# Folding the features of a 2-D Fourier mixing a second time, with GpSimd row copies and permuted transposes

## The chip, the cores and the metric

The kernel runs on one core of a Trainium2 chip. The core has a matrix engine (TensorE, PE in the profile, with its weight loads listed as PEld), a vector engine (VectorE, DVE), a scalar engine (ScalarE, ACT), GpSimd (POOL) and a queue that issues DMAs (SyncE, SP). Each engine takes its instructions in order and waits on semaphores of the others. The metric is the device time of one execution in microseconds. The kernel before takes 1586.29 us (median of 3 runs, 1585.91 to 1588.53).

## The reference

Attention with a sigmoid instead of a softmax, a Fourier mixing, and a feed-forward block. The shapes are 8 batches, 12 heads, 448 tokens and 64 features per head, so 768 features per token and 3072 in the hidden layer, all in float32:

```python
scores = scale * q @ k.T - log(S)          # per batch and head
x = (1 / (1 + exp(-scores))) @ v           # heads side by side: 448 x 768 per batch
u = x + real(fft(fft(x, axis=tokens), axis=features))
un = (u - mean(u)) / sqrt(var(u) + 1e-6)   # per token
out = u + relu(un @ w_ch1) @ w_ch2
```

The real part of the two-dimensional transform is cos·cos − sin·sin over tokens and features. Both the cosine and the sine have symmetries, so that sums and differences of mirrored rows ("folds") halve a dimension before the tables are multiplied on.

## The kernel before

There are three stages. **Attention and mixing** runs from 0 to about 400 us. Twenty-four groups `gg` (8 batches of 3) hold 4 heads each. A group is 8 time steps `t` of a loop that goes in twos: at part 0 the half-size scores of this group and the last products with v of the group before, at parts 1 to 3 the scores (`scores`, three matmuls of a float32 split in a high part `hi`, made by ScalarE, and a low part `lo`, made by VectorE in `rest`), each followed by a sigmoid on ScalarE. A table `extra` (filled by `at(t, fn)`) says which other work is written into which step: the loads, the casts, the scanning and repacking of the feed-forward weights (`weight`, four VectorE instructions per tile, lines 310 to 319), the folds, and the layer norm of the first 512 tokens (`norm`, with the steps of `norm_plan`). After each step `pin()` fixes the order on every engine, so an engine's order is that of the program text.

**The mixing of a batch** starts when its three groups are done. `values` leaves the attention output transposed in `xT`: six tiles `p` of 128 features (two heads each), each with 2 x 225 tokens, which already are the two mirrored token halves. `fold` works on GpSimd: level 0 adds and subtracts tile `p` and tile `p + 3` (features 384 apart), level 1 the two token halves, and the last level the mirrored tokens; the result goes to `xp`. These are 6 instructions for each of 3 pairs of tiles, 18 for a batch. Then `mix_units(b)` gives a list of TensorE pieces: `stage_d` multiplies with the feature table `cd_sb` (K = 384 features, hence 3 matmuls in a row, for two parities of 193 columns, times 2 x 2 combinations: 24 matmuls `psd` for a batch); ScalarE copies the result to `A`, interleaving the parities; `stage_s` multiplies with the token table (4 matmuls `pss` of 385 columns); VectorE makes the sum `sm` and the difference `df`; `add_x` transposes `xT` back (`psx`, 8 times 3 transposes) and VectorE adds, for the second half of the features with a reversed read of `sm` or `df`, into `u`, which a DMA writes to `u_dram`.

The list holds end marks, and `mix_some()` runs the pieces up to the next mark once per group, at part 2. So three groups in a row carry the **first, second and third section** of a batch's mixing: 13 `psd` and 2 `pss`; 11 `psd` and 9 transposes; 2 `pss` and 15 transposes. The last batch has no groups left to hide in: its pieces alternate with the first up-projections (`psh`) of the next stage, in `mix_rest` and `fill`. The units of a batch are put on the list at step 24 b + 34.

**The plain stage** (to about 590 us) does the feed-forward block of the first 512 tokens while it prepares the weights (`pair`: ScalarE and VectorE split them in two halves, lines 456 and 458, GpSimd makes differences, line 466). **The fast stage** does the other six chunks with seven products instead of eight for each 2 x 2 block. Its matmuls are `psf` and `pso`.

`norm_plan` has ten steps. Step 7 scales the rows (VectorE, line 399), step 8 makes the high half `hl` (ScalarE, line 422), step 9 the low half (VectorE, line 426) and issues two transposing DMAs. `hl` has one buffer. `fx` and `xp` are pools of buffers; `w5` is a one-buffer tag there.

## Time and profile before

| what | value |
|---|---|
| runs | 1586.29 us (1585.91 to 1588.53) |
| the profiled execution | 1584.93 us, its span 1583.2 us |
| mean granted TensorE clock | 0.999 |
| PE busy | 1557.6 us, 98% of the span |
| DVE busy | 1278.7 us, 81% |
| ACT busy | 655.6 us, 41% |
| POOL busy | 319.0 us, 20%, none of it after 570 us |
| DMA | 402.43 MB, 254 GB/s |

A float32 matmul appears as two records in the profile, so the 192 `psd` of the program are 384 records. The records of matmuls are pipelined: the pitch from one start to the next is the time that the engine needs, not the mean duration of one record. Some records are missing. In a timeline a row merges neighbouring equal instructions, "x24" gives their number, and the bracket says how long the engine idled before the row and who ended it. In a view of one source line three numbers with slashes are the shortest, the median and the longest instance in nanoseconds.

### The profile page before, as it was taken

How to read it: one execution, taken by the hardware profiler on the slowest of the kernel's cores; microseconds unless marked ns; L12 is line 12 of the kernel's file. 1: busy time of each engine (PE TensorE's matmuls, PEld its weight loads, DVE VectorE, ACT ScalarE, POOL GpSimd, SP SyncE). 2: the span in 40 equal slices, each digit the busy share in tenths (PEclk: the TensorE clock that was granted, in tenths of full speed). 3: DMA queues.
4: the chain of work that ended last, by engine and by line, in shares of the span. 5: the costliest groups of instructions: out<-in, count | busy, mean ns of one | idle time of the engine just before them, and what ended most of it. 6: DMA issues, size and time to landing. Idle time of an engine off the chain costs nothing.

```text
span 1583.2 us, 27410 instructions
## 1 busy us (share of the span) xinstructions
PE 1557.6 (98%) x11059; PEld 1063.7 (67%) x11059; DVE 1278.7 (81%) x2354; ACT 655.6 (41%) x780; POOL 319.0 (20%) x244
## 2 busy tenths in 40 slices
PE   8999999899999999999999999999999999999998
PEld 3556565465555557777777777777777777777775
DVE  4997788793799956887888888888788878877778
ACT  8777777674555424222232233232423232223221
POOL 3644343255788920000000000000000000000000
PEclk9999999999999999999999999999999999999999
DMA  7888878792788977668657766866676777576571
GB/s 296 305 315 275 311 263 296 268 302 88 278 281 295 317 306 291 201 238 303 234 190 291 252 232 229 306 205 253 255 257 196 280 285 241 165 293 255 198 272 50
DMA packets 130399, 402.43 MB, mean 254 GB/s; under 512 B 68832, under 2 KB 70112, under 8 KB 111712
## 3 DMA queue, kind: packets, MB, share of 16 engines
q1 hardware_dynamic: 130272, 400.68, 71.0%
q8 instruction: 86, 1.41, 0.3%
q14 instruction: 41, 0.34, 0.1%
HBM read 311.39 MB, written 73.92 MB: 243 GB/s over the span
## 4 chain that ended last, share of the span: by engine, by line
PE 67%; DVE 4%; DMA 1%; issue 1%; ACT 1%; POOL 1%; SPq 0%; DVEq 0%; ACTq 0%; POOLq 0%
PE pso L897 29%; PE psf L841 29%; PE po L625 4%; PE psh L605 3%; DVE wp L458 1%; DMA ws<-w_dram 1%; DVE F L847 1%; POOL wq L466 1%; DMA U<-u_dram 0%; DVE H L847 0%; ACT H L876 0%; DVE ur L646 0%; DVE ur L925 0%; DVE acc L974 0%; DVE acc L912 0%
## 5 line engine op out<-in xcount | busy, mean ns | idle before, releaser
L841 PE MATMUL psf<-ut,ws 128*128 128x256 f16 x4536 | 506.6, 273 | 2.3 <-DVE ur L646 1.2
L897 PE MATMUL pso<-ws,H 128*128 128x384 f16 x3024 | 503.4, 326 | 1.0 <-DVE H L847 0.9
L841 PEld LDWEIGHTS <-ws 128*128 128x128 f16 x4536 | 443.2, 98 | 62.2 <-issue 1.7
L897 PEld LDWEIGHTS <-H 128*128 128x128 f16 x3024 | 295.3, 98 | 190.2 <-DVE H L847 1.7
L866 ACT ACTIVATE F<-F 128x1024 f32<-128x1024 f32 x72 | 76.1, 1057 | 406.6 <-DVE F L847 406.6
L912 DVE TENSOR_TENSOR acc<-pso,acc 128x384 f32<-128x384 f32 x399 | 207.9, 551 | 19.6 <-PE pso L897 19.6
L847 DVE TENSOR_TENSOR H<-F,H 128x1024 f16<-128x1024 f32 (+1 forms) x144 | 155.4, 1088 | 48.8 <-ACT H L876 48.5
L876 ACT ACTIVATE H<-F 128x1792 f16<-128x1792 f32 x72 | 122.2, 1697 | 110.7 <-DVE F L847 110.7
L127 ACT ACTIVATE a<-sc 128x900 f32<-128x900 f32 x168 | 147.1, 920 | 47.9 <-PE sc L139 47.0
L847 DVE TENSOR_TENSOR F<-X,psf 128x256 f32<-128x256 f32 x288 | 117.2, 419 | 59.3 <-PE psf L841 54.7
L466 POOL TENSOR_TENSOR wq<-wq 128x384 f32<-128x384 f32 x96 | 148.7, 1555 | 37.6 <-DVE wp L458 31.9
L847 DVE TENSOR_TENSOR F<-F 128x256 f32<-128x256 f32 x288 | 109.5, 422 | 24.8 <-ACT F L866 20.1
L177 PE MATMUL av<-a,vr 128*64 128x450 f32 x576 | 119.1, 550 | 0.0
L458 DVE SCALAR_TENSOR_TENSOR wp<-wq,wsc,wp 128x1536 f16<-128x1536 f32 x48 | 98.5, 2085 | 20.7 <-ACT wp L456 20.7
L847 DVE TENSOR_TENSOR X<-X,psf 128x256 f32<-128x256 f32 x216 | 89.9, 416 | 19.0 <-PE psf L841 17.5
L605 PE MATMUL psh<-ut,wp 128*128 128x512 f16 x432 | 98.5, 379 | 0.0
L197 POOL TENSOR_TENSOR eo<-xT 128x450 f32<-128x450 f32 x48 | 53.3, 1132 | 209.3 <-ACT xT L185 209.3
L855 ACT ACTIVATE X<-psf 128x256 f32<-128x256 f32 x72 | 27.8, 386 | 156.4 <-PE psf L841 156.4
L625 PE MATMUL po<-wp,hh 128*128 128x256 f16 (+1 forms) x384 | 88.6, 326 | 0.0
L456 ACT ACTIVATE wp<-wq,wsc 128x1536 f16<-128x1536 f32 x48 | 73.4, 1569 | 27.7 <-DMA wq<-t_dram 25.9
L177 PEld LDWEIGHTS av<-a,vr 128*64 128x64 f32 x576 | 37.2, 136 | 69.1 <-issue 69.1
L605 PEld LDWEIGHTS <-wp 128*128 128x128 f16 x432 | 42.2, 98 | 49.4 <-issue 0.7
(91 smaller groups left out, 1604.6 us busy)
## 6 DMA issues: line engine op xcount, KB each, us to landing
ws<-w_dram SPq DMA_DIRECT2D x144, 1344.0 KB, 7.6
wr<-w_in SPq DMA_DIRECT2D x48, 768.0 KB, 7.8
w_dram<-wp SPq DMA_DIRECT2D x24, 1344.0 KB, 9.9
qk<-qk_in SPq DMA_DIRECT2D x23, 898.0 KB, 6.0
t_dram<-wt SPq DMA_DIRECT2D x48, 384.0 KB, 7.1
wq<-t_dram SPq DMA_DIRECT2D x24, 768.0 KB, 6.5
vr<-v_in SPq DMA_DIRECT2D x24, 448.0 KB, 4.6
U<-u_dram SPq DMA_DIRECT2D x24, 384.0 KB, 9.2
```

Source lines behind the costliest of these rows:

```text
L127: nc.scalar.activation(a, ps[:, :, :SQ], AF.Sigmoid, bias=-math.log(S), scale=1.0 / math.sqrt(D))
L177: nc.tensor.matmul(ps[j * D:(j + 1) * D, :SQ], vr[:, h:h + D], a[:, j], start=False, stop=(c == 2))
L458: nc.vector.scalar_tensor_tensor(out=w[:, 1, part], in0=t, scalar=sc, in1=w[:, 0, part], op0=ALU.mult, op1=ALU.subtract)
L466: nc.gpsimd.tensor_tensor(out=t[:, o], in0=t[:, x], in1=t[:, y], op=op)
L605: nc.tensor.matmul(hs[c, f], l[:, m], r[:, m], start=(m == n == 0), stop=(m == NCC - 1 and n == 2))
L625: nc.tensor.matmul(po[n][:, at:at + hi - lo], l[:, cols], r[:, lo:hi], start=(f == 0 and m == 0 and at == 0), stop=(f == NFC - 1 and m == ...
L841: nc.tensor.matmul(ps[:, :TH], w[:, x, a, m * 128:(m + 1) * 128], ut[y][:, b, m], start=(m == n == 0), stop=(m == n == 2))
L847: nc.vector.tensor_tensor(out=o, in0=x, in1=y, op=op)
L866: nc.scalar.activation(F[:, 0:4], F[:, 0:4], AF.Relu)
L876: nc.scalar.activation(hts[P][:, 0], F[:, 1:8], AF.Copy)
L897: nc.tensor.matmul(ps[:, :384], H[:, x, a, tp * 128:(tp + 1) * 128], w[:, y, b], start=(j == n == 0 and half != 1), stop=(j == 1 and n == ...
L912: later(0, lambda: nc.vector.tensor_tensor(out=to, in0=ps[:, :384], in1=to, op=ALU.add))
```

## The change

It has four parts.

1. **The features are folded once more.** The host permutes the heads (`HEADS`), the features of four heads of v, and the rows and columns of the weights and of the result (`_columns`), so that mirrored features meet in one partition. `fold` gets a level 2 that combines pair 2 with pair 1. K falls from 384 to 256, so `stage_d` has 2 matmuls in a row instead of 3 (16 for a batch), and its table has two parities of 198 columns instead of 193 (`NL` = 396). The `pss`, `A`, `Q`, `sm` and `df` have 396 columns instead of 385.
2. **GpSimd copies rows.** The fold leaves four rows in the wrong partition (0 or 64). `turn_rows` rotates them with four copies of 1 x 900 elements for each batch.
3. **Permuted transposes replace column handling.** The second half's transposes multiply with a permuted identity (`perm`, a new DMA of 128 x 384) and the tables hold the columns in the order wanted. ScalarE's copy to `A` is now contiguous, and the reads of `sm` and `df` are runs of 64 columns and not a reversed row.
4. **The norm's halves come later**: steps 8 and 9 at 23 + 16 j and 25 + 16 j instead of 19 + 8 j and 22 + 8 j. The row of the weight scan takes the `w5` buffer, and `weight_row` moves from step `TP` + 2 to `TP` + 4.

The order of the folds changes with `FOLDS`: the last level of pairs 0 and 1 now stands behind the row copies, and pair 2 has eight instructions. On GpSimd the first batch reads as follows before (`eo` is level 0, `fd` level 1, `xp` the result):

```order
L197 TENSOR_TENSOR eo<-xT 128x450 x2
L200 TENSOR_TENSOR fd<-eo 128x450 x2
L203 TENSOR_TENSOR xp<-fd 128x4x113 x2
L197 TENSOR_TENSOR eo<-xT 128x450 x2
L200 TENSOR_TENSOR fd<-eo 128x450 x2
L203 TENSOR_TENSOR xp<-fd 128x4x113 x2
L197 TENSOR_TENSOR eo<-xT 128x450 x2
L200 TENSOR_TENSOR fd<-eo 128x450 x2
L203 TENSOR_TENSOR xp<-fd 128x4x113 x2
```

and as follows after the change:

```order
L206 TENSOR_TENSOR eo<-xT 128x450 x2
L209 TENSOR_TENSOR fd<-eo 128x450 x2
L206 TENSOR_TENSOR eo<-xT 128x450 x2
L209 TENSOR_TENSOR fd<-eo 128x450 x2
L223 COPY eo<-fd 1x900
L223 COPY fd<-fd 1x900 x2
L223 COPY fd<-eo 1x900
L215 TENSOR_TENSOR xp<-fd 128x4x113 x2
L206 TENSOR_TENSOR eo<-xT 128x450 x2
L209 TENSOR_TENSOR xp<-eo 128x450 x2
L212 TENSOR_TENSOR xp<-xp,fd 128x2x225
L212 TENSOR_TENSOR xp<-xp,fd 128x450
```

followed by the two last-level instructions of pair 2. There are 18 tensor instructions as before and four copies; behind the last `xT` of the batch stand eight instructions and not six.

On TensorE the first section of the first batch, between the scores, reads before:

```order
L139 MATMUL sc<-hi,lo 128x450 x2
L216 MATMUL psd<-cd_sb,xp 113x193 x12
L227 MATMUL pss<-A,cs_sb 113x385
L216 MATMUL psd<-cd_sb,xp 113x193
L227 MATMUL pss<-A,cs_sb 113x385
```

and after:

```order
L144 MATMUL sc<-hi,lo 128x450 x2
L235 MATMUL psd<-cd_sb,xp 113x198 x8
L245 MATMUL pss<-A,cs_sb 113x396
L235 MATMUL psd<-cd_sb,xp 113x198
L245 MATMUL pss<-A,cs_sb 113x396
```

Four `psd` have left; the second section loses four as well.

On ScalarE the first high half `hl` of the norm stands before between the cast of the weights (`wt`) and the copy of a group's attention output, a few instructions ahead of the mixing's copies `A`:

```order
L127 ACTIVATE a<-sc 128x900
L185 ACTIVATE xT<-av 128x450
L127 ACTIVATE a<-sc 128x900 x2
L305 ACTIVATE wt<-wr 128x768
L422 ACTIVATE hl<-un 128x768
L185 ACTIVATE xT<-av 128x450
```

and after, half a group later, behind them:

```order
L239 ACTIVATE A<-psd 113x396 x2
L132 ACTIVATE a<-sc 128x900 x2
L120 ACTIVATE hi<-qk 128x898
L324 ACTIVATE wt<-wr 128x768
L441 ACTIVATE hl<-un 128x768
L132 ACTIVATE a<-sc 128x900
```

It moved past a section of the mixing, and the second of the two stands 16 steps behind the first instead of 8.

The diff, cut to its core:

```diff
-FOLDS = ((12, 13, 14, 15, 16, 17), (20, 21, 22, 23, 24, 25), (28, 28, 28, 29, 29, 29))
+FOLDS = ((12, 0, 0), (13, 0, 1), (14, 0, 2), (15, 0, 3), (20, 1, 0), (20, 1, 1), (21, 1, 2), (21, 1, 3), (27, 0, 6), (27, 0, 7),
+         (28, 2, 0), (28, 2, 1), (28, 2, 2), (28, 2, 3), (29, 2, 4), (29, 2, 5), (29, 2, 6), (29, 2, 7))
+NB = 66
+NL = 6 * NB
...
-            cd_sb = c1.tile([128, 2, 2, 3, 193], F32, name="cd_sb")
+            cd_sb = c1.tile([128, 2, 2, 2, NL // 2], F32, name="cd_sb")
+            perm = c1.tile([128, 3, 128], F32, name="perm")
...
                 elif lv == 1:
-                    eo, fd = eos[p]
-                    e.tensor_tensor(out=fd[:, n], in0=eo[:, :, 0], in1=eo[:, :, 1], op=op)
+                    eo = eos[p]
+                    e.tensor_tensor(out=fd[:, 2 * n:2 * n + 2], in0=eo[:, :, 0], in1=eo[:, :, 1], op=op)
+                elif lv == 2:
+                    k = slice(1, 3) if n else slice(0, 4, 3)
+                    e.tensor_tensor(out=fd[:, k], in0=fd[:, k], in1=fds[b][:, 1, k], op=op)
                 else:
-                    fd = eos[p][1]
+                    fd = fd.rearrange("p (c r) n -> p c r n", c=2)
                     e.tensor_tensor(
-                        out=xp[:, n, :, :, p], in0=fd[:, :, :, 0:HM], in1=fd[:, :, :, HS - 1:HM - 2:-1], op=op)
+                        out=xp[:, n, :, :, 1 - p // 2], in0=fd[:, :, :, 0:HM], in1=fd[:, :, :, HS - 1:HM - 2:-1], op=op)
+
+            def turn_rows(b, n):
+
+                z, y = fds[b][:, 0], fds[b][:, 1]
+                s = eos[1].rearrange("p k r n -> p (k r) n")
+                o, x = ((s[64:65], y[64:65]), (y[64:65], y[0:1]), (y[0:1], z[64:65]), (z[64:65], s[64:65]))[n]
+                nc.gpsimd.tensor_copy(out=o, in_=x)
...
                     nc.tensor.matmul(
-                        ps[:HM, par * 193:par * 193 + 193], xp[:, kp ^ c, c, par, p],
-                        cd_sb[:, c, par, p], start=(p == 0), stop=(p == 2))
-                    if par == 1 and p == 2:
+                        ps[:HM, par * NL // 2:(par + 1) * NL // 2], xp[:, kp ^ c, c, par, p],
+                        cd_sb[:, c, par, p], start=(p == 0), stop=(p == 1))
+                    if par == 1 and p == 1:
                         act_next.append(lambda: nc.scalar.activation(
-                            A[:, kp, c].rearrange("s (i r) -> s r i", r=2),
-                            ps[:HM, 0:386].rearrange("s (r i) -> s r i", r=2), AF.Copy))
+                            A[:, kp, c], ps[:HM, 0:NL], AF.Copy))
...
-                        ps[:m, :385], cs_sb[:HM, kp, c, :m], A[:, kp, c, :385], start=True, stop=True)
+                        ps[:m, :NL], cs_sb[:HM, kp, c, :m], A[:, kp, c], start=True, stop=True)
...
-                    for i in range(3):
+                    for i, (j, n) in enumerate((((0, 0), (1, 0), (2, 0)), ((3, 1), (5, 2), (4, 2)))[hf]):
                         nc.tensor.transpose(
-                            ps[:HM - kp, i * 128:(i + 1) * 128], xT[:, hf * 3 + i, r, kp:HS:2], ident)
-                    y = d if hf == r else s
+                            ps[:HM - kp, i * 128:(i + 1) * 128], xT[:, j, r, kp:HS:2], perm[:, n])
-                    ysl = y[:m, 384:0:-1] if hf else y[:m, 0:384]
+                    y = (d if hf == r else s)[:m].rearrange("s (r b k) -> s b r k", r=2, k=NB)
+                    y = y[..., 0:64] if hf else y[..., 2:66]
...
-                    return [(0.33, lambda par=par, p=p: stage_d(kp, c, par, p)) for par in range(2) for p in range(3)]
+                    return [(0.33, lambda par=par, p=p: stage_d(kp, c, par, p)) for par in range(2) for p in range(2)]
...
-                    for n, t in ((1, 10), (7, 17), (8, 19 + 8 * j), (9, 22 + 8 * j)):
+                    for n, t in ((1, 10), (7, 17), (8, 23 + 16 * j), (9, 25 + 16 * j)):
...
+                for n in range(4):
+                    at(24 * b + 22, lambda b=b, n=n: turn_rows(b, n))
```

More of the change, by code (lines that the diff above doesn't have):

```diff
@@ L26 @@
 CP = 128
+HEADS = [0, 5, 4, 3, 1, 2, 6, 11, 10, 9, 7, 8]
 CH = 64
@@ L543, in spectral_attention_ffn @@
             at(17, lambda: nc.sync.dma_start(cd_sb, cd))
-            at(22, lambda: (nc.sync.dma_start(cs_sb, cs), nc.sync.dma_start(ident, ident_in)))
+            at(22, lambda: (nc.sync.dma_start(cs_sb, cs), nc.sync.dma_start(ident, ident_in[:, 0]),
+                            nc.sync.dma_start(perm, ident_in[:, 1:])))
             ends = sorted([(t, (-10, -5, -1, 0, 3)) for t in range(15, TP, 8)]
@@ L1027, in _layout @@
     B = q.shape[0]
+    q, k, v = (a[:, HEADS] for a in (q, k, v))
+    v = v.copy()
+    for h in (2, 3, 8, 9):
+        v[:, h] = v[:, h][..., -np.arange(D) % D]
+    w1, w2 = w1[_columns()], w2[:, _columns()]
     qt, kt = (a.reshape(B, 2, NG, 2, S, D).transpose(0, 2, 1, 3, 5, 4).reshape(B, 2 * NG, 2 * D, S) for a in (q, k))
@@ L1060, in _layout, with _heads, _places, _columns @@
     return {"qk_in": qk, "v_in": vt, "w1_in": w1t, "w2_in": w2t, "cd_in": cd, "cs_in": cs,
-            "id_in": np.eye(128, dtype=np.float32)}
+            "id_in": np.stack([np.eye(128, dtype=np.float32)] + [
+                np.eye(128, dtype=np.float32)[:, p.ravel()] for p in _places()], axis=1)}
+def _heads():
+    import numpy as np
+    r = np.arange(64)
+    p = np.arange(128)
+    return np.stack([np.concatenate([r, 320 + r]), np.where(p % 64, 320 - p, 256 - p), 64 + p])
+def _places():
+    import numpy as np
+    res = np.zeros((3, 2, 64), int)
+    for k in range(2):
+        core = np.array([n for n in range(2, 128) if n % 64 > 1 and n % 2 == k])
+        ends = np.array([k, 64 + k])
+        res[0, k] = np.concatenate([core, ends])
+        res[1, k] = np.concatenate([(128 - ends) % 128 if k else ends, 128 - core])
+        res[2, k] = np.concatenate([ends, core])
+    return res
+def _columns():
+    import numpy as np
+    l, p = _heads(), _places()
+    half = [l[b][p[0].ravel()] for b in range(3)]
+    return np.concatenate(half + [384 + l[b][p[n].ravel()] for b, n in ((0, 1), (2, 2), (1, 2))])
 def _tokens():
```

56 lines of the change are left out of this document (32 added, 24 removed).

## The prediction

> **What bounds the kernel now.** I read the busy shares first, then the chain that ended last, then how the stage that the change touches looks in a timeline of TensorE, and the waits of that stage.
>
> ```profile
> PE 1557.6 (98%) x11059; PEld 1063.7 (67%) x11059; DVE 1278.7 (81%) x2354; ACT 655.6 (41%) x780; POOL 319.0 (20%) x244
> PE 67%; DVE 4%; DMA 1%; issue 1%; ACT 1%; POOL 1%; SPq 0%; DVEq 0%; ACTq 0%; POOLq 0%
> ```
>
> TensorE is busy for 98% of the span and carries the chain of waits. Whether the attention stage, the first 400 us, is bound by it too is read from its rhythm. These rows, from the timeline of TensorE, are the half-size scores that open every third group, each at the same place of a batch:
>
> ```profile
> 81.60 0.93 PE L152 MATMUL sc<-qk 64*64 64x450 f32 x8
> 128.71 0.94 PE L152 MATMUL sc<-qk 64*64 64x450 f32 x8
> 175.80 0.94 PE L152 MATMUL sc<-qk 64*64 64x450 f32 x8
> 223.65 0.94 PE L152 MATMUL sc<-qk 64*64 64x450 f32 x8
> 271.56 1.22 PE L152 MATMUL sc<-qk 64*64 64x450 f32 x7
> 324.39 1.00 PE L152 MATMUL sc<-qk 64*64 64x450 f32 x8
> ```
>
> Two batches take 47.11 and 47.09 us, equal to 0.02 us: TensorE sets the pace and nothing interrupts it. The next three take 47.85, 47.91 and 52.83, so something does there. Behind 400 us no edit changes an instruction of the main loop, and I take it as moved, not changed. So the gain is what TensorE gets rid of in the attention stage, plus those interruptions, minus what VectorE and GpSimd do to it.
>
> **The matmuls.** This is the first section of a batch:
>
> ```profile
> 105.14 4.19 PE L216 MATMUL psd<-cd_sb,xp 128*113 128x193 f32 x24
> 109.17 0.81 PE L227 MATMUL pss<-A,cs_sb 113*113 113x385 f32 x2
> 109.82 0.49 PE L216 MATMUL psd<-cd_sb,xp 128*113 128x193 f32 x2
> L216 PE MATMUL psd<-cd_sb,xp x384: 323/327/420, 57.7 to 399.4; 128*113 128x193 f32 x192
> ```
>
> From start to start, 24 records of `psd` take 109.17 − 105.14 = 4.03 us, 0.168 us each, and 2 records of `pss` take 0.65 us, 0.325 each. (The means of single records overlap and aren't used.) The slope is (0.325 − 0.168) / (385 − 193) = 0.00082 us per column. Of 384 records of `psd` 128 go: −21.5 us. The 256 that stay get 5 columns: 256 x 0.0041 = +1.05 us. The 64 records of `pss` get 11 columns: 64 x 0.009 = +0.6 us. Sum: **−19.9 us**, 2.5 us per batch, 1.25 in each of two sections.
>
> Of the **last batch** half is not earned. Its pieces run among the first up-projections, and there TensorE waits for something that the change doesn't touch:
>
> ```profile
> 377.52 1.92 POOL L197 TENSOR_TENSOR eo<-xT 128x450 f32<-128x450 f32 x2 [5.72 <-ACT xT L185]
> 381.52 2.08 POOL L203 TENSOR_TENSOR xp<-fd 128x452 f32<-128x452 f32 x2
> 384.15 2.13 PE L216 MATMUL psd<-cd_sb,xp 128*113 128x193 f32 x12
> 389.76 3.04 ACT L456 ACTIVATE wp<-wq,wsc 128x1536 f16<-128x1536 f32 x2 [2.92 <-DMA wq<-t_dram]
> 393.25 0.90 PE L227 MATMUL pss<-A,cs_sb 113*113 113x385 f32 x2 [2.73 <-ACT A L220]
> ```
>
> GpSimd finishes `xp` at 383.60, half a microsecond ahead of the first `psd`. With two more instructions of 0.98 behind the last `xT` it finishes 2 us later, and `psd` starts some 1.6 us late. Yet four pieces further `pss` stands at 393.25 behind two weight casts of 3.04 us on ScalarE, which wait for a DMA. The lateness and the shorter first section both vanish in that wait of 2.73 us: **+1.3 us** (nothing, if the DMA lands earlier; 2.6, if the row copies below are at their upper price).
>
> **The norm's halves.** These rows, ScalarE and TensorE mixed, lie in the long batches:
>
> ```profile
> 216.71 0.84 ACT L422 ACTIVATE hl<-un 128x768 f16<-128x768 f32 x1 [2.60 <-DVE un L399]
> 220.91 0.59 PE L248 MATMUL psx<-ident,xT 128*113 128x128 f32 x3 [0.55 <-ACT A L220]
> 281.45 0.84 ACT L422 ACTIVATE hl<-un 128x768 f16<-128x768 f32 x1 [2.80 <-DVE un L399]
> 285.62 0.90 PE L248 MATMUL psx<-ident,xT 128*112 128x128 f32 x3 [1.93 <-ACT Q L231]
> 300.58 0.84 ACT L422 ACTIVATE hl<-un 128x768 f16<-128x768 f32 x1 [3.28 <-DMA ut<-hl]
> 304.78 0.90 PE L227 MATMUL pss<-A,cs_sb 113*113 113x385 f32 x2 [1.53 <-ACT A L220]
> 271.00:304.00 33.00, 29.61 (x181) 16.66 (x181) 27.22 (x41) 21.43 (x29) 7.91 (x9) 0.95 0.67 218
> ```
>
> The last is the row of that stretch, with the granted clock at 0.95. Three times ScalarE stands for 2.6 to 3.3 us in front of the high half `hl`, for a scaling that VectorE hasn't done or for the transposing DMAs that still read the one buffer; what is queued behind it (the copies `xT`, `Q` and `A`) comes late, and TensorE waits. The cost is 47.85 − 47.10 = 0.75 and 52.83 − 47.10 = 5.73 us, **−6.5 us** in all. The 0.8 us of the batch from 223.65 is another wait (VectorE's small norm instructions, not moved) and stays. After the change `hl` comes six steps behind the scaling (before: two), and the second 16 steps behind the first (before: eight), two thirds of a batch of 47.1 us, so 31 us. The 0.84 us of work stays on ScalarE, which is busy for 23 of 33 us there (the row from 172 us below): nothing. Bounds: 2 us if one of the waits only moves, 7.3 if the 0.8 goes as well.
>
> **VectorE in the first 90 us.** A gain of TensorE is only kept while the others can follow:
>
> ```profile
> 20.00:57.00 37.00, 35.63 (x244) 16.12 (x240) 31.18 (x32) 32.21 (x42) 25.14 (x18) 1.00 0.86 323
> 57.00:74.00 17.00, 16.96 (x108) 10.09 (x108) 16.69 (x21) 11.31 (x17) 8.68 (x6) 1.00 0.82 283
> 74.00:90.00 16.00, 16.00 (x115) 10.16 (x111) 15.61 (x20) 12.75 (x18) 8.50 (x7) 1.00 0.93 309
> 172.00:205.00 33.00, 32.51 (x214) 19.35 (x212) 28.25 (x46) 23.36 (x31) 14.09 (x14) 1.00 0.86 319
> PEld sc L139 <- DVE lo L123: 0.7, 2, 0.3
> L319 DVE SCALAR_TENSOR_TENSOR wt<-wr,wt x48: 957/958/1728, 29.2 to 351.4; 128x768 int32<-128x768 int32 x48
> L310 DVE TENSOR_SCALAR_CACHE_REDUCE wt<-wt x48: 937/945/949, 25.9 to 347.5; 128x768 f32<-128x768 f32 x48
> L197 POOL TENSOR_TENSOR eo<-xT x48: 976/983/1752, 22.0 to 378.5; 128x450 f32<-128x450 f32 x48
> ```
>
> The columns of the first rows are the stretch, its length and the busy times of PE, PEld, DVE, ACT and POOL. From 57 to 90 us VectorE is busy for 32.3 of 33 us; later for 28 of 33. The scores already wait for its low parts (0.7 us, twice). So what TensorE saves in the first section of the first batch, 1.25 us, is lost: that is the lower bound. The upper bound comes from GpSimd. VectorE's instructions with two inputs from SBUF take 0.96 us alone and up to 1.73 beside GpSimd, whose own go from 0.98 to 1.75; line 310, with one input, never slows down. So the two share something, and each microsecond of GpSimd can cost VectorE 0.77/0.98 = 0.8. Between 36 and 57 us GpSimd gets two level-2 instructions (2.0 us) and four row copies.
>
> A **row copy** of 900 elements in one partition is nowhere in the trace. From below it is the 0.10 us of GpSimd's start-up fills; from above twice the 0.98 of a `tensor_tensor` with 450 results. I take 1.0: a copy of 900 reads as many words as that instruction does. That makes 6.0 us more on GpSimd, 4.8 for VectorE if all of it collides; I take six tenths, since about that share of VectorE's time there is two-input work: 2.7. With the 1.3 it is **+4 us** (1.3 to 6; to 9 with copies of 2 us).
>
> The Trainium skill, page "GPSIMD Engine Reference", section "Specifications", says that GpSimd's way to SBUF is shared with VectorE and that instructions of VectorE with two SBUF inputs contend; the rows above agree, and this speaks against putting copies there. Its section "Elementwise — side-by-side cycle accounting" gives about 1.03 cycles per element for one input against 2.6 for two: an estimate by that page of 0.8 us for a copy, by which this term would be 3.6 us instead of 4; no run here shows it yet.
>
> In later batches the fold has room:
>
> ```profile
> 75.29 2.63 POOL L197 TENSOR_TENSOR eo<-xT 128x450 f32<-128x450 f32 x2 [8.58 <-ACT xT L185]
> 89.48 2.58 POOL L197 TENSOR_TENSOR eo<-xT 128x450 f32<-128x450 f32 x2 [6.06 <-ACT xT L185]
> 94.13 2.09 POOL L203 TENSOR_TENSOR xp<-fd 128x452 f32<-128x452 f32 x2
> ```
>
> The last pair starts at 89.48 and `psd` at 105.14: 15.7 us for eight instructions of 1.0 to 1.3. GpSimd idles 6 to 9 us before each pair, more than four copies of 1 us.
>
> **Hand-offs.** With `psd` shorter, ScalarE's copy `A` has less cover:
>
> ```profile
> 106.31 0.95 ACT L115 ACTIVATE hi<-qk 128x898 fp32r<-128x898 f32 x1
> 107.40 0.53 ACT L220 ACTIVATE A<-psd 113x386 f32<-113x386 f32 x1
> ```
>
> The first four `psd` will end at about 106.7, but `hi` holds ScalarE to 107.26; `A` ends at 107.8, and the `pss` that reads it is due at 105.14 + 8 x 0.344 = 107.9. No wait, or 0.2 us: **+0.7 us** for seven batches (0 to 1.5). The contiguous copy, the eleven columns on VectorE and its runs of 64 lie on engines with slack after 90 us; the table's DMA shrinks by 732 words per row, the permutations add 384. I cost these at nothing; without slack 64 additions of perhaps 0.05 us more would be 3 us.
>
> **The sum**: −19.9 + 1.3 − 6.5 + 4 + 0.7 = −20.4 us. The span goes from 1583.2 to 1562.8 us and the profiled execution from 1584.93 to 1564.5. The median of the runs lies 1.4 us above the profiled one, so 1586.3 − 20.4 = **1566 us**. The bounds all at once give 1560 (−26) and 1577 (−9); the forecast's own range is 1560 to 1573, without the upper price of the copies.
>
> **Rivals.** *GpSimd's collisions decide*: copies of 2 us (its upper bound) make the early term 9 us, and the batches after it lose 1 us each: 20.4 − 5 − 7 = 8.4 us gain, 1578. For it: two engines that visibly slow each other, and VectorE at 86% (28.25 of 33). Against it: that leaves it 4.75 us of slack in 33, and four copies come once in 47. *The norm's wait only moves*: `hl` keeps its one buffer. Gain 13.9, 1572. *VectorE catches up at once*: no early loss but 1.3, no hand-off waits: gain 24, 1562 or a little below. *Slower*: from the `xT` of pair 1 (75.29) to `psd` (105.14) there are 29.9 us, 28.5 with the shorter section, for 14 tensor instructions of about 1.25 and four copies: up to (28.5 − 17.5) / 4 = 2.75 us per copy nothing happens; above it each microsecond costs 4 us per batch, because `psd` waits for GpSimd. The gain of 2.5 per batch and 0.8 from the norm is used up at 3.6 us; at 4 us eight batches lose 40 us, less the gain, and the kernel takes about 1604. For it: no GpSimd copy and no one-partition instruction in the trace. Against it: nothing on GpSimd takes over 2.6 us, collisions included. *The change doesn't do what it says* has nothing for it: the order lists show 16 `psd` per batch.
>
> **Chances.** My forecast (1560 to 1573) 0.67, collisions 0.12, the norm's wait moved 0.09, catching up 0.08, slower 0.04. The range that leaves out two tenths at most is 1560 to 1577. A measurement here tells 0.2%, 3 us, from no change. Faster 0.94, the same 0.02, slower 0.04.
>
> **What would show it.** Right: the opening rows of a batch 44.6 us apart from about 120 us on; no idle time in front of ScalarE's `hl`; copies near 1 us; waits of the scores for `lo` of 2 to 4 us before 75 us. Wrong: `psd` waiting for GpSimd in every batch, a pitch of `psd` that doesn't follow the columns (0.172 us per record is expected), a new idle time in front of `pss`, or a longer main loop behind 400 us.

## The result, and the profile after

The change makes the kernel slower: **1598.55 us** (median of 4 runs, 1596.05 to 1603.23) against 1586.1 us for the kernel before on the same chip, a ratio of 1.0081 (95% interval 1.0066 to 1.0097). The forecast was 1566 us. The profiled execution is the slowest of the four, 1603.23 us with a span of 1601.5 us, 18.3 us more than before, so its stretches show more than the 12.5 us between the medians.

The page of the changed kernel, TensorE's busy time and the granted clock in 40 slices:

```profile
PE 1551.6 (97%) x10931; PEld 1052.8 (66%) x10931; DVE 1304.5 (81%) x2354; ACT 655.0 (41%) x780; POOL 374.3 (23%) x276
PEclk9999998899999999999999999999999999999999
```

TensorE has 128 records less, VectorE is busy 26 us longer with the same 2354 instructions, and GpSimd 55 us longer, with 32 copies more. Before, no slice had a clock below 9 tenths. The opening scores of every third group, from the timeline of TensorE after the change:

```profile
81.95 0.93 PE L157 MATMUL sc<-qk 64*64 64x450 f32 x8
130.86 0.93 PE L157 MATMUL sc<-qk 64*64 64x450 f32 x8
178.66 0.94 PE L157 MATMUL sc<-qk 64*64 64x450 f32 x8
226.44 0.93 PE L157 MATMUL sc<-qk 64*64 64x450 f32 x8
289.74 1.58 PE L157 MATMUL sc<-qk 64*64 64x450 f32 x8
342.29 0.93 PE L157 MATMUL sc<-qk 64*64 64x450 f32 x8
```

Batches of 44.6 us from 120 us on were forecast. They take 47.8, 47.8, 63.3 and 52.6 us; before it was 47.1, 47.9, 47.9 and 52.8. The first `psh` starts 16.6 us later than before (396.86 against 380.26), so the loss lies in the attention stage. What TensorE saves in the first and second section is there: groups of 15.35 and 14.34 us stand where 16.56 and 15.59 stood. The third section gives it back, and two single places add more.

**The third section.** VectorE, GpSimd and TensorE after the change, in the group from 130.86 us (`lo` is the scores' low part, `wt` a weight tile, `u` the mixing's addition; the bracket is idle time and who ended it):

```profile
131.24 0.94 DVE L329 TENSOR_SCALAR_CACHE_REDUCE wt<-wt 128x768 f32<-128x768 f32 x1
132.22 1.30 DVE L333 TENSOR_SCALAR wt<-wt 128x768 int32<-128x768 int32 x1
133.55 1.70 DVE L336 SCALAR_TENSOR_TENSOR wt<-wr,wt 128x768 int32<-128x768 int32 x1
135.28 1.70 DVE L338 SCALAR_TENSOR_TENSOR wt<-wr,wt 128x768 int32<-128x768 int32 x1
141.82 1.62 DVE L338 SCALAR_TENSOR_TENSOR wt<-wr,wt 128x768 int32<-128x768 int32 x1
143.37 0.55 DVE L275 TENSOR_TENSOR u<-psx,df 113x384 f32<-113x384 f32 x1
129.44 2.67 POOL L223 COPY fd<-fd 1x900 f32<-1x900 f32 x2
132.17 0.93 POOL L223 COPY fd<-eo 1x900 f32<-1x900 f32 x1
133.18 2.99 POOL L215 TENSOR_TENSOR xp<-fd 128x452 f32<-128x452 f32 x2
138.73 2.24 POOL L206 TENSOR_TENSOR eo<-xT 128x450 f32<-128x450 f32 x2 [2.56 <-ACT xT L191]
143.97 2.03 PE L266 MATMUL psx<-perm,xT 128*112 128x128 f32 x9 [2.30 <-DVE u L275]
```

The whole group, before (first) and after; the columns are the stretch, its length, the busy time and count of PE, PEld, DVE, ACT and POOL, the granted clock, the DMA share and GB/s:

```profile
128.71:143.65 14.94, 14.44 (x100) 7.78 (x96) 11.67 (x19) 10.78 (x15) 5.92 (x6) 1.00 0.89 300
130.86:148.95 18.09, 15.79 (x99) 8.95 (x95) 17.75 (x23) 10.98 (x15) 15.08 (x12) 0.91 0.80 300
```

GpSimd is busy for 15.1 of 18.1 us where it was 5.9 of 14.9, and VectorE has no room left. VectorE's weight instructions with two inputs take 1.70 us and not 0.96, line 333 takes 1.30 and not 0.56; line 329 keeps its 0.94. So two weight tiles end at 143.4, `u` comes late, and TensorE's transposes, which need the PSUM bank that `u` frees, stand for 2.30 us. Nothing like it stood here before. (Pair 1 has no last level of its own any more, so only pair 0's stands behind the copies.)

The Trainium skill, page "SBUF — State Buffer", section "Who interferes with whom", describes this: VectorE and GpSimd share one pair of ports as an exclusive lock, wanted by VectorE's instructions with two SBUF inputs and by a `tensor_scalar` in its two-port form, but not by the one that writes an accumulator, while ScalarE has ports of its own. The trace agrees in each case (lines 336, 333, 329; ScalarE's is below).

**The clock.** The same place by stretches, with the same columns:

```profile
141.60:143.90 2.30, 0.07 (x1) 0.00 (x0) 2.27 (x4) 0.34 (x1) 2.30 (x2) 1.00 1.05 430
143.90:146.00 2.10, 2.03 (x11) 1.69 (x11) 2.00 (x6) 0.00 (x0) 1.94 (x3) 0.59 1.00 413
146.00:147.20 1.20, 1.20 (x6) 1.09 (x8) 1.20 (x3) 0.00 (x0) 1.12 (x2) 0.50 1.05 435
147.20:148.20 1.00, 1.00 (x12) 0.62 (x9) 1.00 (x2) 0.68 (x1) 1.00 (x1) 0.76 0.93 389
```

After 2.3 us of waiting TensorE runs at 0.5 to 0.76 of its clock for 4.3 us. The third section takes 18.09 us against 14.94 before: 3.15 us, of which the wait is 2.3.

**The norm.** SyncE, VectorE, ScalarE and TensorE after the change, in the batch of 63.3 us:

```profile
255.73 0.41 SPq L341 DMA_DIRECT2D t_dram<-wt  x1
270.20 0.95 DVE L445 TENSOR_TENSOR hl<-un,hl 128x768 f16<-128x768 f32 x1
271.19 0.38 SPq L427 DMA_DIRECT2D un<-u_dram  x1
277.79 0.89 ACT L324 ACTIVATE wt<-wr 128x768 f32<-128x768 f32 x1 [9.42 <-DMA wr<-w_in]
279.17 0.98 PE L266 MATMUL psx<-perm,xT 128*113 128x128 f32 x3 [5.31 <-ACT xT L191]
284.72 0.98 PE L266 MATMUL psx<-perm,xT 128*113 128x128 f32 x3 [4.57 <-DVE u L275]
```

SyncE issues nothing for 15 us. `un` has one buffer. The second pair's load stands at step 96 + 32 + 4 = 132, and the low half that reads the buffer last (line 445) now stands at 96 + 25 + 16 = 137, no longer at 126. The load waits for it, the weights' loads wait behind the load, ScalarE stands for 9.4 us, and this group takes 27.4 us against 16.0. ScalarE's waits in front of `hl` are gone, as forecast.

### The profile page after: what moved, and what is told of

Read it like the earlier page. It is cut to its first block, busy times and chain, and to the rows that moved or that the text cites. A ratio compares the mean times of both kernels' runs of the same rounds, so it can differ in the third digit from the quotient of the medians.

```text
span 1601.5 us, 27187 instructions
## 1 busy us (share of the span) xinstructions
PE 1551.6 (97%) x10931; PEld 1052.8 (66%) x10931; DVE 1304.5 (81%) x2354; ACT 655.0 (41%) x780; POOL 374.3 (23%) x276
## 4 chain that ended last, share of the span: by engine, by line
PE 60%; DVE 9%; DMA 3%; ACT 2%; issue 1%; POOL 1%; SPq 0%; ACTq 0%; DVEq 0%; POOLq 0%
PE psf L862 26%; PE pso L918 25%; PE po L646 4%; PE psh L626 3%; DVE F L868 2%; DMA ws<-w_dram 1%; DVE wp L477 1%; DVE H L868 1%; ACT H L897 1%; DVE acc L933 1%; ACT F L887 1%; DMA U<-u_dram 1%; DVE X L868 1%; POOL wq L485 1%; DMA wq<-t_dram 0%
## 5 line engine op out<-in xcount | busy, mean ns | idle before, releaser
L933 DVE TENSOR_TENSOR acc<-pso,acc 128x384 f32<-128x384 f32 x399 | 207.5, 549 | 19.9 <-PE pso L918 19.9
L477 DVE SCALAR_TENSOR_TENSOR wp<-wq,wsc,wp 128x1536 f16<-128x1536 f32 x48 | 98.9, 2091 | 20.5 <-ACT wp L475 15.2
L868 DVE TENSOR_TENSOR X<-X,psf 128x256 f32<-128x256 f32 x216 | 89.6, 415 | 19.6 <-PE psf L862 17.6
```

Source lines behind the costliest of these rows:

```text
L477: nc.vector.scalar_tensor_tensor(out=w[:, 1, part], in0=t, scalar=sc, in1=w[:, 0, part], op0=ALU.mult, op1=ALU.subtract)
L868: nc.vector.tensor_tensor(out=o, in0=x, in1=y, op=op)
L933: later(0, lambda: nc.vector.tensor_tensor(out=to, in0=ps[:, :384], in1=to, op=ALU.add))
```

## Experiments

The kernel before had medians of 1585.1 to 1587.0 us beside these. The last five columns are starts in the timeline of TensorE: the first scores of four groups, named by where they stand in the kernel before, and the first `psh`. Runs that are not in the table stand in the text. From the first `psh` to the end the profiled executions take 1200.9 to 1205.9 us, though no edit touches the main loop and of the mixing only the last batch lies there, so a difference of a few microseconds between two times needn't lie in the attention stage.

| kernel | us | ratio to before (95%) | 128 us | 175 us | 223 us | 356 us | `psh` |
|---|---|---|---|---|---|---|---|
| before | | | 128.71 | 175.80 | 223.65 | 356.14 | 380.26 |
| after | 1598.55 | 1.0081 (1.0066–1.0097) | 130.86 | 178.66 | 226.44 | 373.20 | 396.86 |
| a_norm_back | 1598.57 | 1.0084 (1.0067–1.0101) | 129.87 | 177.63 | 226.94 | 368.44 | 392.44 |
| b_norm_late | 1589.74 | 1.0028 (1.0016–1.0040) | 128.97 | 176.06 | 223.16 | 362.17 | 386.29 |
| a_no_copies | 1578.83 | 0.9962 (0.9947–0.9976) | 125.21 | 169.84 | 219.15 | 351.14 | 375.12 |
| a_old_order | 1580.30 | 0.9967 (0.9956–0.9979) | 125.32 | 169.95 | 220.99 | 352.39 | 376.31 |
| a_norm_mid | 1594.24 | 1.0051 (1.0036–1.0066) | 130.78 | 178.56 | 226.35 | 364.88 | 388.51 |
| a_mid_no_copies | 1577.08 | 0.9941 (0.9927–0.9956) | 124.28 | 168.93 | 213.60 | 347.94 | 371.56 |
| a_weight_170 | 1572.72 | 0.9912 (0.9897–0.9927) | 124.07 | 168.95 | 213.62 | 346.33 | 369.98 |
| b_copies | 1600.33 | 1.0085 (1.0068–1.0102) | 132.70 | 179.79 | 227.63 | 370.93 | 395.05 |
| a_copies_act | 1598.32 | 1.0076 (1.0060–1.0093) | 132.39 | 180.75 | 229.06 | 367.52 | 391.46 |
| a_behind_q | 1588.36 | 1.0012 (1.0002–1.0021) | 131.02 | 177.24 | 223.81 | 358.69 | 383.14 |
| a_rows_early | 1586.99 | 1.0001 (0.9989–1.0013) | 128.91 | 174.35 | 220.26 | 355.24 | 379.89 |
| a_rows_best | 1587.44 | 1.0000 (0.9992–1.0009) | 126.61 | 171.85 | 217.81 | 354.96 | 379.59 |

### Which part of the change costs

The norm alone, put back in the changed kernel (`a_norm_back`) and put into the kernel before (`b_norm_late`):

```diff
-for n, t in ((1, 10), (7, 17), (8, 23 + 16 * j), (9, 25 + 16 * j)):
+for n, t in ((1, 10), (7, 17), (8, 19 + 8 * j), (9, 22 + 8 * j)):
```

> The changed kernel with the norm's steps 8 and 9 at their old places. Theory 1 (the loss is the norm's: the load of the second pair of rows shares one buffer with the rows whose low half is now later, and SyncE's queue stands behind it for some 15 us): the group that took 27.4 us in the changed kernel falls back to about 16.5, the three waits of ScalarE before the high half (6.5 us) come back, and the stall near 333 us goes if it is a consequence: 1588 us, or 1593 if that stall stays. Rival (the norm's move is a gain of 6.5 us as predicted, and all of the loss lies in the fold): 1605 us.

> The kernel before with only the norm's steps 8 and 9 at their new places. Theory 1: the load of the rows is queued on SyncE behind the late low half here too, 11 us lost at that place and up to 5 behind it against 6.5 gained: 1591 to 1596 us. Rival (the move is the gain that was predicted): 1580 us.

In the kernel before the move costs 4.7 us, where 6.5 us of gain were forecast; the blocked group takes 27.5 us there too. In the changed kernel putting it back gains nothing, neither the 1588 us of theory 1 nor the rival's 1605: the blocked group falls to 17.7 us as theory 1 said, but groups of 21.9 and 19.6 us come up behind it, where ScalarE waits 5.1 us for the transposing DMAs of `hl` and TensorE 3.1 us for a late `u`. So the block is real, and most of the loss lies elsewhere.

The copies, and the order that they bring (both on top of `a_norm_back`; `a_old_order` also puts pair 0's last level at steps 16 and 17):

```diff
-                for n in range(4):
-                    at(24 * b + 22, lambda b=b, n=n: turn_rows(b, n))
```

> The changed kernel with the norm at its old places and without the four GpSimd row copies: four rows of the folded features stay in the wrong partition, so part of the mixing is left out. Theory 2 (GpSimd's copies collide with VectorE in the third section of a batch, VectorE's additions u come 2 to 4 us late, TensorE waits and its clock drops): the waits of the third section's transposes for u are gone, and 3 us for each of seven batches: 20 to 25 us under the kernel with the norm alone put back, 1563 to 1568. Rival (the order: pair 0's last level and pair 2's eight instructions stand in the third section with or without copies): half of the wait stays, 8 to 12 us less, about 1578. Second rival (the permuted transposes or the additions in runs of 64 are slow by themselves): no change, 1588.

> As the kernel without copies, and pair 0's last level stands right behind its first two levels, as in the kernel before. Theory 2 (the copies): the same time as without copies, within 3 us. Rival (the order): another 8 to 12 us less, because GpSimd has 2 to 3 us less to do in the third section.

**The copies cost 19.7 us**, just under the 20 to 25 us that theory 2 expected; the order by itself costs nothing (1580.3 against 1578.8). That 1578.83 us is also the first rival's 1578 is luck: both counted from a kernel of 1588 us, and that took 1598.57. The third section without copies, GpSimd and VectorE:

```profile
124.23 2.96 POOL L215 TENSOR_TENSOR xp<-fd 128x452 f32<-128x452 f32 x2
133.15 2.68 POOL L206 TENSOR_TENSOR eo<-xT 128x450 f32<-128x450 f32 x2 [5.96 <-ACT xT L191]
132.09 0.96 DVE L336 SCALAR_TENSOR_TENSOR wt<-wr,wt 128x768 int32<-128x768 int32 x1
133.08 0.96 DVE L338 SCALAR_TENSOR_TENSOR wt<-wr,wt 128x768 int32<-128x768 int32 x1
135.06 0.56 DVE L275 TENSOR_TENSOR u<-psx,df 113x384 f32<-113x384 f32 x1 [1.03 <-PE psx L266]
```

GpSimd's idle 5.96 us are VectorE's undisturbed ones: the last weight instruction ahead of `u` ends 8.8 us after the group's first scores (134.04 − 125.21), with copies 12.6 us (143.44 − 130.86). VectorE has 1.0 us to spare and loses 3.8. The regular batch takes 44.63 us, the 44.6 of the forecast, so no cost of the permuted transposes or of the additions in runs of 64 is seen.

The same four copies in the kernel before, into a free row:

```diff
+                for n in range(4):
+                    at(24 * b + 26, lambda b=b, n=n: more_copies(b, n))
```

> The kernel before with four GpSimd copies of 1 x 900 elements for each batch, from a row of fd to a free row of eo, in the step behind pair 1's last level, where GpSimd idled for 9 us; the computation is unchanged. Theory 2: VectorE's instructions beside them stretch by 0.8 to 1 us for each copy, 3.2 to 4 us; VectorE had 2.25 us to spare before u, so 1 to 2 us are lost for each of seven batches: 1594 to 1600 us. Rival (copies in GpSimd's idle time are free, as the prediction had it, and the loss belongs to the other edits): 1586 us.

15.2 us. The timeline shows where: in the regular batches nothing is lost (14.93 and 14.94 us for the third sections from 132.7 and 179.8 us). VectorE had more to spare there in the kernel before, as its timeline shows, and GpSimd had the last level of pair 1 behind it:

```profile
138.55 0.56 DVE L255 TENSOR_TENSOR u<-psx,df 113x384 f32<-113x384 f32 x1 [2.25 <-PE psx L248]
```

The 15.2 us are lost in the first batch (3.8 us in its first section) and behind 227 us, where the norm adds to VectorE's work. So the time just above the expected 1594 to 1600 us is luck: the loss of 1 to 2 us in each of seven batches did not come.

### Taking the norm's block away, and what then remains

`a_norm_mid` writes steps 8 and 9 at 23 + 10 j and 25 + 10 j, so that the last low half (step 131) stands ahead of the load (132). `a_mid_no_copies` is that without copies, and `a_weight_170` has in addition

```diff
-          + [(t, (-10, -2, -1, 0, 3)) for t in (34, 58, 82, 154, 162, 178)])
+          + [(t, (-10, -2, -1, 0, 3)) for t in (34, 58, 82, 154, 170, 178)])
```

> The changed kernel with the norm's steps 8 and 9 at 23 + 10 j and 25 + 10 j: as late as in the change for the first half, but the last low half is written one step ahead of the load of the next rows. Theory 1 (the load that stands on SyncE behind the low half is the norm's whole loss, ScalarE's waits are the gain): the 27.4 us group falls to about 16, ScalarE doesn't wait before the high half, 11 us less than the changed kernel and 16 with the stall near 333 us: 1583 to 1588 us. Rival (with VectorE late from the collisions, some wait before the high half comes back as it did with the old places): 1594 to 1598 us.

> The same without GpSimd's four row copies; four rows stay in the wrong partition, so part of the mixing is left out. Theory 2: this is the gain that was predicted, matmuls 19.9 and norm 6.5 us less 1.3, 0.7 and what is left of VectorE's early lateness: 1562 to 1568 us. Rival (the norm's waits move elsewhere also without collisions): 1574 to 1579 us.

> The kernel with the norm at 23 + 10 j and without the row copies (part of the mixing is left out), with the additional weight tile of step 162 moved to step 170. Theory 3 (the one group that still takes 22.0 us instead of 15.5 is a pile-up on VectorE: three weight tiles in steps 159 to 162, ahead of the norm's low half, so that SyncE and the next tile's load come late): that group falls to 16 us, 6 us less, 1570 to 1572 us. Rival (the low half alone, wherever the tiles stand): the stall moves with it or stays, 1575 to 1578 us.

The blocked group takes 17.1 us, so theory 1 holds for it. By the first `psh` `a_norm_mid` is 8.4 us earlier than the changed kernel, by the medians 4.3 us less, and not 11: the stall near 333 us, a group of 21.6 us in the changed kernel, doesn't go with the block (22.0 us; 15.6 before). The times of `a_norm_mid` and `a_mid_no_copies` lie in their rivals' ranges, but no wait in front of `hl` comes back; it is this stall that stays, also without collisions. SyncE, ScalarE and VectorE there, without copies:

```profile
302.48 9.04 SPq L447 DMA_TRANSPOSE ut<-hl  x2
308.50 0.97 ACT L324 ACTIVATE wt<-wr 128x768 f32<-128x768 f32 x1 [4.67 <-DMA wr<-w_in]
308.46 0.96 DVE L338 SCALAR_TENSOR_TENSOR wt<-wr,wt 128x768 int32<-128x768 int32 x1
309.34 0.95 DVE L445 TENSOR_TENSOR hl<-un,hl 128x768 f16<-128x768 f32 x1
```

VectorE works off three weight tiles in a row, the low half comes last, SyncE stands for 9 us before its transposes, and ScalarE waits for a tile's load. With one tile moved eight steps on, that group takes 19.3 us where theory 3 expected 16, so the theory holds in part. The kernel takes 4.4 us less by the medians; of the 5.1 us between the profiled spans only 1.6 are there at the first `psh`, and the rest lies behind it. The four kernels without copies in the table are the only ones faster than before, and they leave the rotation of the rows out.

How much room is left there is seen in the rows by stretch, the last batch before (first) and in `a_weight_170` (second):

```profile
308.84:356.14 47.30, 46.83 (x313) 28.02 (x309) 45.20 (x62) 34.51 (x47) 23.07 (x18) 1.00 0.92 309
```

```profile
295.84:346.33 50.49, 46.26 (x296) 26.06 (x292) 46.23 (x62) 35.27 (x48) 24.93 (x18) 0.97 0.90 307
```

VectorE is busy for 45.2 us in this batch already before, and the DMA engines for 0.92 of it. A batch of 44.6 us can't hold that. From the group at 224 us to that at 356 the kernel before takes 132.5 us, `a_weight_170` 132.7, `a_no_copies` 132.0, `a_old_order` 131.4: there, at most 1.1 us of TensorE's saving is kept. That VectorE and the loads are the limit is argued from these shares; no run took work from them there.

### Can the rows be moved at another price?

All of these have the norm at 23 + 10 j. The first puts the copies on ScalarE, at steps 24 and 26:

```diff
-nc.gpsimd.tensor_copy(out=o, in_=x)
+nc.scalar.activation(o, x, AF.Copy)
```

> The same with the four copies on ScalarE, two in each of the first two steps of the third section's group, and pair 0's last level behind pair 2's level 1; everything is computed. Theory 2 (only the sharing between GpSimd and VectorE made the copies dear): near the kernel without copies, plus up to 0.5 us for each batch where ScalarE's four times 0.9 us push a sigmoid back: 1564 to 1572 us. Rival (any engine that stands in that group is late with these four copies): ScalarE's sigmoids come 2 to 3 us late and the scores wait for them in each batch, 1580 to 1590 us.

```profile
135.37 0.95 ACT L223 ACTIVATE eo<-fd 1x900 f32<-1x900 f32 x1
137.44 0.56 DVE L333 TENSOR_SCALAR wt<-wt 128x768 int32<-128x768 int32 x1
138.04 0.96 DVE L336 SCALAR_TENSOR_TENSOR wt<-wr,wt 128x768 int32<-128x768 int32 x1
145.71 0.59 PE L266 MATMUL psx<-perm,xT 128*112 128x128 f32 x3 [1.92 <-ACT Q L249]
```

Beside ScalarE's copies VectorE keeps its 0.56 and 0.96 us, so the stretching comes with copies on GpSimd and not on ScalarE. But now ScalarE has 3.8 us more to do ahead of its copy `Q`, and TensorE waits for that: 18.7 us for the section. The rival holds in kind (this engine too is late in that group), but it is `Q` and not a sigmoid that comes late, and 1598.32 us is above the rival's 1580 to 1590. Neither engine has room for the copies in that group.

Three kernels then sought room elsewhere: behind `Q` on ScalarE (`a_copies_behind`), as DMAs issued by ScalarE (`a_copies_dma`), two on VectorE and two behind `Q` (`a_copies_split`).

> The changed kernel with the norm at 23 + 10 j, and the four copies on ScalarE directly behind the copy Q of the third section, where ScalarE stood idle for 2.6 to 3.2 us; a spare row is taken from xp, and pair 0's last level stands behind pair 2's level 1. Everything is computed. Theory 2 (what counts is idle time of the copying engine in that group; ScalarE has some only there): the section's wait for u or Q is gone, ScalarE pushes a sigmoid back by about 1.2 us per batch: 1577 to 1587 us. Rival (sigmoids late by four copies, 3 us or more per batch): 1594 to 1600 us.

> The same with the four copies as DMAs that ScalarE issues, one in each of the four steps of the third section's group; everything is computed. Theory 2: no engine pays for 900 elements, the chain ends some 2 us behind the last issue, in time for pair 2's level 2: 1575 to 1580 us, that of the kernel without copies plus the issues. Rival (issuing or landing holds ScalarE or GpSimd up, so that sigmoids or xp are late): 1585 to 1600 us.

> The same with two copies on VectorE in the third section, where it idled for 1.7 us, and two on ScalarE behind Q; everything is computed. Theory 2: each engine has just the room: 1577 to 1583 us. Rival (VectorE has none, since u is late with any addition there): 2 us per batch, 1590 to 1594 us.

They took 1655.42, 1625.19 and 1657.66 us and say nothing on the question: in the program the copies stood behind GpSimd's reads of the same rows, so that these work on rows that are not rotated, and the copying engine waits for GpSimd. Of use is one row of the DMA kernel, ScalarE's queue:

```profile
142.48 0.84 ACTq L223 DMA_DIRECT2D xp<-fd  x1
```

An issue holds ScalarE for 0.8 us, hardly less than the copy's 0.95.

With level 2 and the last levels written behind the copies, on ScalarE (`a_behind_q`) and as six DMAs of SyncE, which save three rows and write them back (`a_rows_sync` at steps 25 and 29; `a_rows_early` at 22 and 26, its first batch on GpSimd), all with the tile at step 170:

```diff
+r = [xts[b][1][p:p + 1, f]... for p, f in ((64, 0), (64, 1), (0, 0))]
+o = (y[64:65], z[64:65], y[0:1])
+for i in range(3):
+    nc.sync.dma_start(*((r[i], o[i]) if n == 0 else (o[i], r[(2, 0, 1)[i]])))
```

> The changed kernel with the norm at 23 + 10 j, the weight tile at step 170, and the four copies on ScalarE behind the copy Q of the third section; this time level 2 and the last levels stand behind the copies in the program, so ScalarE doesn't wait for GpSimd. Everything is computed. The bound below is 1573 us, the kernel without copies. Theory 2 (a copy costs what the copying engine, and VectorE beside GpSimd, can't spare in that group): VectorE isn't stretched, ScalarE has 2.6 us to spare of 3.8, so 1.2 us or a little more for each batch: 1577 to 1587 us. Rival (ScalarE's sigmoids are needed at once behind Q): 3 us or more per batch, 1595 us or more.

> The same with six DMAs on SyncE in place of the copies, three that save the rows in step 25 and three that write them back in step 29; everything is computed. Theory 2 (no engine gives time, a round of DMAs lands 3.6 us behind its issue and xp has 4 us to spare): 1573 to 1580 us. Rival (SyncE, standing before the second three, holds up the weights' loads and stores, or xp comes late): 1585 us or more.

> The kernel with the rows moved by DMAs of SyncE, the saves in step 22 and the writes back in step 26, three steps earlier than in a_rows_sync, where level 2 waited 5.1 us for the rows and TensorE up to 7.7 us for xp; the first batch uses GpSimd copies. Everything is computed. Theory 2 (without an engine's time the copies cost nothing if the rows land before level 2): no wait for xp from the second batch on, 1573 to 1580 us. Rival (SyncE's queue is held up by them, so weights and scores' loads are late): 1590 us or more.

Behind `Q` the third sections take 16.0 us, 1.0 over the bound, as theory 2 said; the first batch, where ScalarE waits for GpSimd, loses 4 us more. 1588.36 us is just over the expected range. `a_rows_sync` took 1606.60 us (1.0127, 1.0111–1.0143): level 2 waited 3.7 to 6.8 us for the rows in the batches up to 260 us, and TensorE up to 7.7 us for `xp`. Three steps earlier the third sections up to 175 us take 14.97 us as without copies, and the regular batch 45.4. So moved by no engine the rows cost the third section nothing. Yet 1586.99 us lies between the two expected ranges, for behind it is this (SyncE and GpSimd in `a_rows_early`):

```profile
222.69 10.89 SPq L454 DMA_TRANSPOSE ut<-hl  x2
233.68 2.52 SPq L230 DMA_DIRECT2D fd<-xp  x3
237.48 2.57 POOL L212 TENSOR_TENSOR xp<-xp,fd 128x450 f32<-128x450 f32 x2 [3.36 <-DMA fd<-xp]
```

The rows stand on SyncE behind the norm's transposes, and the group takes 21.4 us. The last kernel moves these (25 + 8 j, 27 + 8 j) and gives the first batch the change's order:

> As a_rows_early, with two causes of its remaining losses taken away: the norm's steps 8 and 9 at 25 + 8 j and 27 + 8 j, so that the first transposing DMAs stand behind the rows' write-back on SyncE and not ahead of it (there the queue stood for 10.9 us, and TensorE waited for xp, 6 us in that group), and the first batch's folds in the order of the change (TensorE waited 2.6 us for xp there). Everything is computed. If copies without an engine's time and these two queue positions are the causes: 5 and 2 us less, 1580 us, 0.4% under the kernel before. Rival (the waits move to the next thing on SyncE or VectorE): 1585 to 1588 us.

Both named stalls go, 20.57 to 18.24 and 21.41 to 15.36 us. Two others come, 21.2 and 23.4 us, where ScalarE waits 6.1 and 7.0 us for weight loads (`wr`) that SyncE issues only behind the norm's transposes, for which its queue stands 9.1 and 8.6 us. The rival holds: the kernel is even with the one before, not under it.

### Late `u`, or too little time on VectorE?

`a_mix_first` was to write the third section ahead of its step's weight instructions; `a_tile_late` writes the second tile of that group at step 31 instead of 25 (both: copies on GpSimd, norm at 23 + 10 j, tile at 170):

```diff
-          + [(t, (-11, -3, -1, 0, 3)) for t in range(17, TP, 8)]
+          + [(t + 6 * (t % 24 == 1), (-11, -3, -1, 0, 3)) for t in range(17, TP, 8)]
```

> The changed kernel (copies on GpSimd) with the norm at 23 + 10 j, the weight tile at step 170, and with the third section of the mixing written ahead of the weights' instructions of its step, so that VectorE's additions u don't stand behind a stretched weight tile. With the copies as in the change some 1590 us would be expected. Theory 2 in its narrow form (TensorE loses because u stands behind stretched weight instructions on VectorE, and the stretch itself is harmless): the wait for u falls from 2.3 to under 0.5 us in each batch and most of the 17 us comes back: 1574 to 1580 us. Rival (VectorE has no time to spare at all in a batch, so the stretch comes out later, as a late low part of the scores): 1586 to 1592 us.

> As the kernel called a_mix_first (GpSimd copies, norm at 23 + 10 j, weight tile at step 170), in which the edit moved no instruction of VectorE, since both weight tiles stand a step ahead of the third section. Here the second tile of each third-section group is written behind the section (step 31 instead of 25), so that u stands directly behind the scores' low part. Theory 2 in its narrow form (u is late only because a stretched tile stands ahead of it): the wait of 2 us or more with its slow clock is gone in the groups from 128 us on, 3.1 us for each of them, and 15 us or more come back: 1575 to 1580 us. Rival (VectorE has no time to spare over a whole batch): the wait comes back as one for the low part or for sm and df in the next group, 1590 to 1597 us.

`a_mix_first` (1594.80 us, 1.0056, 1.0039–1.0073) changed no order on VectorE in that section, since both tiles already stand a step ahead, so it only repeats the kernel with copies: the wait for `u` is still 2.0 us, and the tile's move gains nothing beside copies (1594.24 without it). In `a_tile_late` (1599.84 us, 1.0083, 1.0066–1.0100) the wait for `u` is gone, the section of 18.1 us takes 15.8, and the next groups take 17.5 and 15.6 instead of 15.3 and 14.3. SyncE and ScalarE there:

```profile
154.21 2.75 SPq L313 DMA_DIRECT2D wr<-w_in  x2
158.46 0.93 ACT L324 ACTIVATE wt<-wr 128x768 f32<-128x768 f32 x1 [3.10 <-DMA wr<-w_in]
```

SyncE issues nothing from 142.1 to 154.2 us; then come two weight loads, ScalarE's cast waits 3.1 us for one, its copy `A` stands behind the cast, and TensorE waits 1.5 us for `A`. The narrow form fails, since the time doesn't come back. But the rival's waits, for the low part or for `sm` and `df`, aren't what comes: a load is late, and the edit moved the tile's load and cast as well. Whether VectorE lacks time over the whole batch, or only order, stays open.

## Why the prediction was wrong, by its steps

**Matmuls, −19.9 us: right in size, earned for half the stage.** Timeline of TensorE after:

```profile
157.54 2.94 PE L235 MATMUL psd<-cd_sb,xp 128*113 128x198 f32 x16
160.32 0.83 PE L245 MATMUL pss<-A,cs_sb 113*113 113x396 f32 x2
```

16 records from start to start in 2.78 us are 0.174 us each, forecast 0.172. Without copies the group at 224 us starts 10.0 us earlier (213.62 against 223.65), all of four batches' 2.5 us. Behind it, see above, next to nothing is kept; VectorE's 45.2 of 47.3 us in the last batch and the late loads are the likely reason. The prediction looked at VectorE's share only up to 304 us (27.2 of 33) and put the long batch of 52.83 us down to the norm's waits alone.

**The step that failed: "In later batches the fold has room", and the term of 2.7 us for GpSimd's extra work.** That term stood for 6.0 us on GpSimd in the first batch alone, 4.0 of them copies, so the copies' share is 1.8 us (4.8 times six tenths is 2.9, a slip of 0.2); the later batches were put at nothing. The idle 6 to 9 us of GpSimd are real, and the copies' median time, 0.93 to 1.15 us, was right:

```profile
L223 POOL COPY fd<-fd x16: 927/932/1686, 40.4 to 389.1; 1x900 f32<-1x900 f32 x16
L223 POOL COPY eo<-fd x8: 926/938/2342, 39.0 to 385.7; 1x900 f32<-1x900 f32 x8
```

What was not asked is what VectorE does in that idle time. It does its stretchable work there and ends 3.8 us later, and the third section has 1.0 us of slack by then, not the 4.75 of 33 that a stretch of two groups gave. That more than the two-input instructions stretch stood in the trace of before, in the view of line 314 (333 after), which has one input (shortest, median and longest in ns):

```profile
L314 DVE TENSOR_SCALAR wt<-wt x48: 547/560/1468, 26.9 to 348.4; 128x768 int32<-128x768 int32 x48
```

The copies cost 17.2 us (1594.24 − 1577.08) instead of 1.8.

**VectorE in the first 90 us, +4**: at the group from 96.56 us the changed kernel is 4.6 us late and had been due 2.5 us early, so 7.1 us are lost; without copies 1.5 (`a_no_copies`) and 0.5 (`a_mid_no_copies`). By the two pairs of kernels that differ only in them, the copies cost 4.7 and 6.5 us up to here, against 1.8. The wait of the scores for `lo` came as forecast (2.2 us, up to 59.87 us).

**The norm, −6.5: failed.** The waits in front of `hl` went, but a step that is moved takes its buffer's next load with it, and on SyncE everything behind that. The prediction checked `hl`'s single buffer and not `un`'s. Alone the move costs 4.7 us, and the block in the changed kernel costs 4.3 (1598.55 − 1594.24).

**Last batch, +1.3**: the wait of `psd` for `xp` came (2.12 us, 1.6 forecast), but not the saving beside it. With its share of the matmuls, −2.5, this batch was to take 1.2 us less; from the first `psh` to the first `psf` it is 208.5 us against 208.3. **Hand-offs, +0.7**: 44.63 us for a batch without copies, no new wait in front of `pss`; right or smaller. From the first `psf` to the end it is 996.1 us against 994.6, within the 993.5 to 996.1 of the table's kernels down to `a_copies_act`, so the main loop is unchanged as far as the traces tell.

**Rivals.** "GpSimd's collisions decide" was the right mechanism with 1 us per later batch; 3.15 us were measured, because a late `u` also costs the clock. "The norm's wait only moves" was right in that a wait moved, but it moved to `un`'s buffer and not to `hl`'s, which the rival named. The slower rival (`psd` waiting for GpSimd) is near in time and wrong in cause: `psd` waited 2.4 us for `xp` in all, twice.

Of the 32.6 us between forecast and median the runs explain 19.7: 15.4 for the copies (17.2 less 1.8) and 4.3 for SyncE's block. The other 12.9 us are a remainder. Its place is shown: without copies and block (`a_mid_no_copies`) the group at 224 us comes 10.05 us earlier, but from there to the first `psh` the kernel takes 1.35 us more than before, where 13 less were forecast (7.5 for the matmuls of three batches, 5.7 for the norm). Its cause is argued. The tile moved to step 170 takes 4.4 us off without copies and nothing beside them, it is no part of the change, and it was not moved in the kernel before, so it is no term of this sum.

## What to carry to other kernels

Before work is put into an engine's idle time, look at what its neighbour on the same ports does in just that time, and count the neighbour's slack in that group and not its mean over a longer stretch. When a step is moved later, follow the buffer that it frees to the next load, and that load's queue to all that stands behind. In the batch where VectorE was busy for 95% before, a shorter TensorE earned nothing.

## What the runs showed of the hardware that was not expected

- TensorE's clock fell after a wait of only 2.3 us, to 0.59 and then 0.50, and was back after 4.3 us. The Trainium skill, page "TensorE: Matmul & The Clock Gate", section "What's actually happening", gives one idle window of about 3.4 us, free-running, for the drop; the wait here is shorter, and in the next batch the clock fell in the same way, to 0.58 and 0.50. The length of the wait alone doesn't decide: behind the wait of 2.73 us at 393.25 us of the kernel before, the clock stays at 1.00, and behind a wait of 3.7 us for `xp` in the last batch it is 1.00 in `a_rows_early` (387.64 us) and 0.50 in `a_rows_best` (387.33 us).
- A copy of one row of 900 elements takes 0.93 us on GpSimd at best (at most 2.34) and 0.95 on ScalarE; as a DMA its issue alone takes ScalarE 0.8 us.
- Beside GpSimd, instructions of VectorE of 0.56 and 0.96 us both grew by 0.74 us in the group shown, and by 0.91 and 0.83 us at most in the whole run (lines 333 and 336): what was added didn't grow with the instruction's own length.
